# A transformer block with recurrent memory, forward and backward: buffers of a tile's input-gradient parts, two banks for the turned score gradient, casts on ScalarE, order of rows, and split loads

## The chip, the core and the metric

The kernel runs on one core of a Trainium2 chip. The core has five engines, each with its own queue of instructions taken in order: TensorE (PE; its weight loads are listed apart as PEld), VectorE (DVE), ScalarE (ACT), GpSimd (POOL) and SyncE (SP, which here only issues DMAs). They wait for one another through semaphores. The metric is the device time of one launch in microseconds (us), lower is better. PSUM, into which TensorE writes, has eight banks of 128 partitions x 512 fp32 numbers; here five are handed out under the name `ps`, two under `fx`, one under `po`.

## The reference

The launch computes the output of one transformer block and the gradients of nine inputs. Cut to what matters:

```python
def _A_ref(x, mem0, Wq, Wk, Wv, Wo, seg_len):      # S 2048, Dm 448, H 16, Dh 256, M 8, seg 32
    mem = mem0
    for s in range(n_seg):                          # 64 segments, L = M + seg_len = 40 rows each
        xs = x[:, s * seg_len:(s + 1) * seg_len, :]
        h = jnp.concatenate([mem, xs], axis=1)
        q, k, v = (einsum('btd,dhe->bhte', h, W) for W in (Wq, Wk, Wv))
        p = softmax(where(mask, einsum('bhqe,bhke->bhqk', q, k) * scale, -1e9))
        o = einsum('bhte,hed->btd', einsum('bhqk,bhke->bhqe', p, v), Wo)
        mem = o[:, :M, :]
        outs.append(o[:, M:, :])
...
h = x + _A_ref(layernorm(x), mem0, Wq, Wk, Wv, Wo, seg_len)
h2 = h + (silu(layernorm(h) @ w_gate) * (layernorm(h) @ w_up)) @ w_down
_out, _vjp = jax.vjp(_f, A_x, A_mem0, A_Wq, A_Wk, A_Wv, A_Wo, B_w_gate, B_w_up, B_w_down)
return (_out, *_vjp(grad_out))
```

All arrays are bfloat16. The memory rows of a segment come from the segment before, so the forward pass is a chain of 64 segments, and the backward pass is another, from the last segment to the first.

## The kernel before

Four stages follow one another. The **forward chain** loads all attention weights into SBUF (Wq, Wk, Wv, Wo, some 15 MB; L424 to L430), takes segment after segment, and keeps rows for the backward pass in DRAM. The **feed-forward stage** runs forward and backward of the second half, eight groups of two tiles of 128 rows. The **backward chain** goes through the segments from 63 to 0. The **tail** reads what was kept and forms the weight gradients, as long accumulations on TensorE.

Tiles are scheduled by a framework that takes instructions by priority. What stands under `k.prio.crit()` goes first; the rest is laid into the holes that the planner sees. The order of each engine's queue is fixed when the program is built. `tc.issue_after(x)` places an instruction behind x. A tile under a tag waits until one of the tag's buffers is free, that is, until every reader of an earlier tile in it has run.

One segment s of the backward chain (r is its place in its tile t of four segments; r runs 3, 2, 1, 0):

- L1163: 128 matmuls give the gradient of the attention output, transposed, in four banks; four copies (DVE, ACT, DVE, ACT) bring it to `doT`.
- L1172: 16 transposes make it token-major, in two halves; L1173 copies the halves to `dO_sb`, the first on DVE, the second on ACT.
- L1181: 32 matmuls give the gradient of the probabilities (`pD`); L1188 to L1193 on DVE form from it and the probabilities `P_sb` the score gradient `dS_bd` (prod, row sum, prod, product with the block-diagonal `P_bd`).
- `heads("v")`, `heads("k")`, `heads("q")`: 16 matmuls each (L1140, in `head_mm`) into three banks. Each bank is copied in two parts, the segment's own 32 rows into `blk` and the 8 memory rows into `lo`; the banks alternate between DVE and ACT (L1202, L1205; all `k.evac` copies show as L75 on DVE and L76 on ACT).
- between "k" and "q", L1221 turns `dS_bd` into one bank `pT`, and two copies bring its halves to `dST_bd`, which `heads("q")` needs.
- `rows_in` (L1212): 32 matmuls for each of v, k and q add the own rows into the bank `pH`; four of them lie side by side on the array.
- L1230 (DVE) and L1231 (ACT) copy `pH` to `om`; L1234 multiplies it by `sel`; L1238 writes the next segment's memory rows to `do_roll`, for which the next segment's L1163 waits; L1245 copies the remaining 24 columns into `dxT`, a buffer for the whole tile.

Not in the critical order: the load of a segment's rows (`load_seg`, L1080 to L1095: V transposed, Q and K on SP, P on POOL into one of two buffers `Pb`, and POOL's two copies into `P_bd`), the stores of `blk` and `lo` on POOL, and at r = 0 the tile's end: 96 matmuls with the memory rows (L1279, into a bank `fx`, q first, then k and v), a copy `om2` (L1282), L1286, two copies into `dxT`, four transposes of `dxT` (L1294) and a LayerNorm backward step (`ln_bwd`, L253 to L264). `lo` has two buffers for v and k and one for q.

At the start of the forward chain POOL issues the loads of Wq, Wk, Wv, Wo and of the remaining rows of x; `rest_rows(0)` (L486) copies rows on POOL as well; SP issues the first rows of x, a store of normalised rows (L459) and the mask (L194, L195), which DVE reads at L413. `rest_unit` (L475) uses two `fx` banks for each of eight units, copied by DVE and ACT.

Of the kernel before, what the change touches and what calls it, by code (L numbers as in the profile page):

```python
# [9 lines left out]
FP32 = mybir.dt.float32  # L10
BF16 = mybir.dt.bfloat16
# [4 lines left out]
P = 128  # L16
# [129 lines left out]
def run_all(k: _K):  # L146
# [17 lines left out]
    k.A = _Arena(arena, "arA", 64.5)  # L164
# [205 lines left out]
def forward_chain(k: _K):  # L370
# [52 lines left out]
    for Wd_sb, Ws, rest in ((Wq_sb, k.Wq2, 0), (Wk_sb, k.Wk2, 64), (Wv_sb, k.Wv2, None)):  # L423
        nc.gpsimd.dma_start(out=Wd_sb, in_=Ws[0:3 * P, :].rearrange("(kc p) n -> p kc n", p=P))  # L424
        if rest is not None:
            nc.gpsimd.dma_start(out=Wqk3[rest:rest + 64, :], in_=Ws[3 * P:D, :])
    for b in range(2):
        nc.gpsimd.dma_start(out=Wv3[64 * b:64 * b + 64, :].rearrange("p (m c) -> p m c", c=512), in_=v3[:, :, b])
    nc.gpsimd.dma_start(out=Wo_sb, in_=k.Wo2.rearrange("(c p) d -> p c d", p=P))
    nc.gpsimd.dma_start(out=xn_all[:, 2:NT, 0:D], in_=x_rows[:, 2:NT])  # L430
# [49 lines left out]
    def rest_rows(s):  # L480
        R = R_b[(s // 8) % 2]
        for dst, src in ((qT_b[s % 2], R[0]), (kT_b[s % 2], R[1])):
            d4 = dst.rearrange("p (c g x) n -> p g c x n", g=2, x=2)
            s4 = src[:, :, M * (s % 8):M * (s % 8) + M].rearrange("p (g c x) n -> p g c x n", g=2, x=2)
            for g in range(2):
                nc.gpsimd.tensor_copy(out=d4[:, g, :, :, 0:M], in_=s4[:, g])  # L486
# [556 lines left out]
def backward_chain(k: _K):  # L1043
# [21 lines left out]
    dh_h = [B(9.875, 448).bitcast(FP32), A(48.5, 448).bitcast(FP32)]  # L1065
    dhx = A(62.5, KC, P)
    dmr = A(63.5, KC, 16, M)
    P_bd, dS_bd, dST_bd = [B(1.25 * i, 8, 2, L) for i in range(3)]
    Pb = [B(3.75 + 0.625 * i, 8, L) for i in range(2)]
# [12 lines left out]
    def load_seg(s):  # L1082
# [8 lines left out]
        P_sb = Pb[s % 2]  # L1091
# [51 lines left out]
    for s in range(NSEG - 1, -1, -1):  # L1143
# [6 lines left out]
        P_sb = Pb[s % 2]  # L1150
# [5 lines left out]
        with k.prio.crit():  # L1156
# [11 lines left out]
            def token_major(hf):  # L1168
# [4 lines left out]
                k.evac(dO_sb[:, 8 * hf:8 * hf + 8, :], ph.rearrange("p (c n) -> p c n", n=P), "vs"[hf])  # L1173
# [19 lines left out]
            nc.vector.tensor_tensor(out=dS_bd, in0=prod.unsqueeze(2).to_broadcast([P, 8, 2, L]), in1=P_bd, op=ALU.mult)  # L1193
# [3 lines left out]
            def heads(nm, lhs, rhs):  # L1197
                pps[nm] = [k.ps1() for _ in range(3)]
                head_mm(pps[nm], lhs, rhs, nm != "v")
                for b in range(3):  # L1200
                    c0, n, v = c12(pps[nm][b], b)
                    k.evac(blk[nm][:, c0:c0 + n, r * SEG:(r + 1) * SEG], v[:, :, M:L], "vsv"[b])  # L1202
                for b in range(3):
                    c0, n, v = c12(pps[nm][b], b)
                    k.evac(lo[nm][:, c0:c0 + n, r * M:(r + 1) * M], v[:, :, 0:M], "svs"[b])  # L1205
                if s == 0:
                    k.tl.outs(*{"v": (7, 9), "k": (9, 10), "q": (10, 11)}[nm], 0, 6)


# [5 lines left out]
            heads("v", dO_sb, P_bd)  # L1215
            rows_in("v", WvT_sb, 0, MC)
            heads("k", Q_sb, dS_bd)
            pT = k.ps1()
            for h in range(8):
                for g in range(2):  # L1220
                    nc.tensor.matmul(pT[64 * g:64 * g + L, h * L:(h + 1) * L], lhsT=dS_bd[:, h, g, :],  # L1221
                                     rhs=ident[:, 64 * g:64 * g + L], start=True, stop=True, skip_group_check=True)
            for g in range(2):
                k.evac(dST_bd[64 * g:64 * g + L, :, g, :],
                       pT[64 * g:64 * g + L, 0:8 * L].rearrange("p (h n) -> p h n", n=L), "vs"[g])
            rows_in("k", WkT_sb, 0, 20)
            heads("q", K_sb, dST_bd)
            rows_in("k", WkT_sb, 20, MC)
            rows_in("q", WqT_sb, 0, MC)
            k.last_om = nc.vector.tensor_copy(out=om[:, 0:224], in_=pH[:, 0:224])  # L1230
            nc.scalar.copy(out=om[:, 224:D], in_=pH[:, 224:D])  # L1231
# [7 lines left out]
            else:  # L1239
                pm0 = k.ps1()  # L1240
                nc.tensor.matmul(pm0[0:M, 0:D], lhsT=sel[:, 24:32], rhs=om[:, 0:D], start=True, stop=True)
                dm = B(3.75, D)[0:M, :]
                nc.vector.tensor_copy(out=dm, in_=pm0[0:M, 0:D])
                nc.sync.dma_start(out=OUT2[:, :], in_=dm)
            nc.scalar.copy(out=dxT[:, :, r * SEG + M:(r + 1) * SEG], in_=pm3[:, :, 0:24])  # L1245
# [301 lines left out]
```

## Time and profile before

| | |
|---|---|
| median of 3 runs | 3059.83 us (3057.76 to 3062.02) |
| the profiled execution | 3052.22 us, span from first to last instruction 3050.5 us, mean granted TensorE clock 0.993 |
| forward chain | 0 to about 1050 us |
| feed-forward stage | about 1050 to 1344 us |
| backward chain | 1344.1 (first L1163) to 2392.6 us |
| tail | to 3050.5 us |
| busy share of the span | PE 95%, PEld 57%, DVE 45%, ACT 35%, POOL 22% |

A segment of the backward chain can be followed by the starts of L1163's first matmul: 15.90, 15.91, 16.78, 15.87 us in turn for most tiles, the third being the one with L1286 and L1294 in it. The first segment of the chain lasts 25.0 us, the next three 16.52, 15.55 and 15.93 us.

How to read the lines: in a timeline, start, length (both in us), engine, line of the kernel, operation, tile written <- tiles read, shapes, count, and in brackets how long the engine had been idle before it and what released it. Buffers are named by their arenas: `arW` (weights, loaded rows), `arA` and `arB` (work), `psf` (a bank of the tag `ps`), `omb` (`om`). A run of instructions of the same kind is one line; its length runs from the first start to the last end, so that neighbouring matmul lines overlap. Ends of matmuls are modelled; starts are measured.

### The profile page before, as it was taken

The numbers are of one execution on the slowest core, as the hardware profiler recorded it, in microseconds if no ns is written. First come the engines' busy times: TensorE is split into PE (matmuls) and PEld (weight loads), VectorE is DVE, ScalarE is ACT, GpSimd is POOL, SyncE is SP. The second block draws the span as 40 slices with busy tenths as digits, with TensorE's granted clock in tenths as the row PEclk, the third lists the DMA queues.
The fourth block names the chain that finished last, engine by engine and source line by source line (L and its number), as shares of the span: only waits on it lengthen the run. The fifth ranks groups of instructions, "written<-read, shape, count | busy, mean of one in ns | idle before, by whom it ended". The sixth has DMA issues, their size and how long they took to land.

```text
span 3050.5 us, 108244 instructions
## 1 busy us (share of the span) xinstructions
PE 2890.3 (95%) x47650; PEld 1748.7 (57%) x47650; DVE 1363.8 (45%) x3437; ACT 1052.6 (35%) x2562; POOL 685.2 (22%) x1522
## 2 busy tenths in 40 slices
PE   6899999999998999989999999999999999999999
PEld 3555555555554555556776677677767554544444
DVE  3555455555555576754555554555455201111110
ACT  2444444444444544443333333333333101111110
POOL 2222222222222232232212122122211112111111
PEclk9999999999999999999999999999999999999999
DMA  7567756776766989895446545455544898959951
GB/s 247 138 168 183 187 165 169 184 178 172 192 173 173 283 217 237 205 326 131 138 130 161 134 131 146 139 141 145 139 138 130 277 285 233 223 173 219 214 160 54
DMA packets 738650, 551.88 MB, mean 181 GB/s; under 512 B 600788, under 2 KB 633732, under 8 KB 735620
## 3 DMA queue, kind: packets, MB, share of 16 engines
q1 hardware_dynamic: 686804, 393.58, 52.5%
q0 software_dynamic: 51376, 151.38, 14.9%
q8 instruction: 374, 6.13, 0.9%
q14 instruction: 96, 0.79, 0.1%
HBM read 169.84 MB, written 236.00 MB: 133 GB/s over the span
## 4 chain that ended last, share of the span: by engine, by line
PE 76%; issue 7%; DVE 6%; DMA 5%; ACT 4%; POOL 1%; SPq 1%; ACTq 0%; POOLq 0%; DVEq 0%
PE psf L1388 8%; PE po L1212 7%; PE psf L1163 7%; PE psf L546 6%; PE psf L663 5%; PE po L708 4%; PE psf L901 4%; PE psf L1140 3%; PE fx L1279 3%; PE fx L1388 3%; PE psf L1234 2%; PE fx L475 2%; PE fx L1025 2%; DVE arA L75 2%; PE psf L560 2%
## 5 line engine op out<-in xcount | busy, mean ns | idle before, releaser
L75 DVE CAST arA<-psf 128x256 bf16<-128x256 f32 (+3 forms) x925 | 422.2, 477 | 768.2 <-PE psf L1388 249.9
L76 ACT CAST arA<-psf 128x96 bf16<-128x96 f32 (+5 forms) x923 | 359.8, 411 | 1052.0 <-PE psf L1163 223.8
L1212 PE MATMUL po<-arW,arA 128*32 128x448 bf16 x6144 | 346.6, 355 | 7.7 <-DMA arW<-Tq 5.5
L1388 PEld LDWEIGHTS <-arA 128*128 128x128 bf16 x1440 | 139.1, 98 | 161.4 <-issue 6.1
L1212 PEld LDWEIGHTS <-arA 128*32 128x32 bf16 x6144 | 158.6, 96 | 125.3 <-issue 6.5
L1163 PEld LDWEIGHTS <-arW 128*128 128x128 bf16 x8192 | 212.8, 96 | 24.0 <-issue 24.0
L1388 PE MATMUL psf<-arW,arA 128*128 128x512 bf16 x882 | 223.3, 382 | 0.0
L1163 PE MATMUL psf<-arA,arW 128*128 128x40 bf16 x8192 | 216.2, 179 | 5.5 <-DVE arA L1238 5.1
L663 PE MATMUL psf<-arW,arA 128*64 128x512 bf16 x1536 | 216.5, 382 | 0.0
L546 PE MATMUL psf<-arW,arA 128*32 128x512 bf16 x3072 | 193.6, 385 | 12.5 <-DVE arA L749 12.5
L76 ACT COPY arA<-psf 128x512 bf16<-128x512 bf16 (+3 forms) x206 | 149.2, 725 | 118.3 <-DVE arA L75 76.5
L76 ACT CAST arB<-psf 128x64 bf16<-128x64 f32 (+3 forms) x384 | 121.9, 318 | 159.7 <-PE psf L550 109.7
L708 PE MATMUL po<-arW,arA 128*32 128x256 bf16 (+1 forms) x4096 | 141.6, 263 | 10.4 <-DVE arA L75 7.7
L75 DVE COPY arA<-psf 128x512 bf16<-128x512 bf16 (+2 forms) x204 | 104.3, 512 | 99.8 <-PE psf L560 55.5
L901 PE MATMUL psf<-arW 128*128 128x256 bf16 (+1 forms) x1288 | 146.3, 274 | 1.3 <-DVE arA L967 0.7
L901 PEld LDWEIGHTS <-arW 128*128 128x128 bf16 (+1 forms) x1344 | 102.4, 97 | 51.5 <-issue 40.8
L546 PEld LDWEIGHTS <-arA 128*32 128x32 bf16 x3072 | 70.4, 96 | 90.2 <-DVE arA L749 18.1
L1140 PEld LDWEIGHTS <-arW 128*128 128x128 bf16 x2048 | 84.3, 99 | 62.1 <-issue 53.2
L1428 PE MATMUL psf<-arW 128*128 128x448 bf16 x525 | 112.1, 356 | 4.5 <-DVE arA L75 4.5
L475 PE MATMUL fx<-arA,arW 128*128 128x64 bf16 (+1 forms) x2048 | 84.2, 195 | 31.7 <-ACT arB L76 19.0
L708 PEld LDWEIGHTS <-arA 128*32 128x32 bf16 x4096 | 93.7, 96 | 32.6 <-DVE arA L75 10.9
L1465 POOL DMA_DIRECT2D out_dram<-arA x96 | 52.1, 545 | 262.6 <-DVE arA L75 237.1
(292 smaller groups left out, 4577.6 us busy)
## 6 DMA issues: line engine op xcount, KB each, us to landing
arW<-T SPq DMA_DIRECT2D x256, 128.0 KB
X_o<-arA SPq DMA_DIRECT2D x37, 512.0 KB
T<-arA SPq DMA_DIRECT2D x64, 256.0 KB
X_v<-arA POOLq DMA_DIRECT2D x30, 512.0 KB, 4.6
X_k<-arA POOLq DMA_DIRECT2D x30, 512.0 KB, 3.8
X_q<-arA POOLq DMA_DIRECT2D x30, 512.0 KB, 3.9
out_dram<-arA POOLq DMA_DIRECT2D x84, 128.0 KB, 4.2
VG<-arA SPq DMA_DIRECT2D x64, 160.0 KB
```

The costliest lines, as they stand in the source:

```text
L75: return nc.vector.tensor_copy(out=out, in_=in_)
L76: return nc.scalar.copy(out=out, in_=in_)
L475: nc.tensor.matmul(banks[w][:, i * 64:(i + 1) * 64], lhsT=lhsT, rhs=xr[lo:hi, kc, :], start=(kc == 0 and i == 0), stop=(kc == KC - 1), ski ...
L546: nc.tensor.matmul(banks[w][32 * q:32 * q + 32, :], lhsT=hT_roll[:, kc, sl, M:L], rhs=(Wq_sb, Wk_sb)[w][:, kc, col(q, b)], start=(kc == 0) ...
L663: nc.tensor.matmul(pV[b][64 * g:64 * g + 64, 0:512], lhsT=hT_flat[:, kc, sl * L:sl * L + 64], rhs=Wv_sb[:, kc, n * 512:(n + 1) * 512], sta ...
L708: nc.tensor.matmul(pO[32 * q:32 * q + 32, 0:w], lhsT=xblk[:, j, r * SEG:(r + 1) * SEG], rhs=Wo_sb[:, cj(j), 256 * dh:256 * dh + w], start= ...
L901: nc.tensor.matmul(ps[fp][:, f2 * 256:(f2 + 1) * 256], lhsT=Wt[lo:hi, kc, c * P:(c + 1) * P], rhs=xT[lo:hi, kc, :], start=(kc == 0 and f2 ...
L1140: nc.tensor.matmul(ps[b][:, i * 2 * L:(i + 1) * 2 * L], lhsT=lhs[:, at, :], rhs=rhs_bd[:, cl // 2, :, :].rearrange("p g n -> p (g n)"), st ...
L1163: nc.tensor.matmul(pss[b][:, jj * L:(jj + 1) * L], lhsT=WoT_sb[:, kc, c * P:(c + 1) * P], rhs=do_roll[:, kc, sl, :], start=(kc == 0), stop ...
L1212: nc.tensor.matmul(pH[32 * (j % 4):32 * (j % 4) + 32, 0:D], lhsT=blk[nm][:, j, r * SEG:(r + 1) * SEG], rhs=WT[:, cj(j), :], start=(nm == " ...
L1388: k.last_mm = nc.tensor.matmul(pa[i][:, 0:w], lhsT=lhs_of(b)[:, i // 2 * P:(i // 2 + 1) * P], rhs=rhs_of(q, b, i % 2), start=(b == 0), sto ...
L1428: k.last_mm = nc.tensor.matmul(pa[i][:, 0:D], lhsT=lhs_of(b, i), rhs=rhs_of(b), start=(bi == 0), stop=(bi == m + 3))
```

## The change

Eight edits, all but the last in the backward chain:

1. The parts of `dxT` for r = 3, 2, 1 go to buffers of their own (`dx3`, `dx2` in three pieces, one of them in the mask tile, `dx1`), copied from the bank in the segment that makes them; at r = 0 POOL copies all five pieces into `dxT`.
2. The third bank of `heads("q")` at r = 3 has its memory rows copied to `lq3` (in the tile `mv2`), and POOL brings them to `lo["q"]` at r = 2.
3. One buffer `P_sb` instead of two; the arena `arA` grows by 0.25 KB.
4. `dO_sb`: the first half on ACT, the second on DVE.
5. All own rows of v, and all memory rows of v, are copied on ACT; for k and q the same bank's own and memory rows stay on one engine, and the memory rows come after the turned copies.
6. The turned score gradient has two banks, one for each half.
7. 12 of the key rows instead of 20 stand before `heads("q")`; `om` is one DVE copy.
8. Start: the weight loads are split between SP and POOL; the copies of `rest_rows(0)` move from POOL to DVE.

```diff
-    for Wd_sb, Ws, rest in ((Wq_sb, k.Wq2, 0), (Wk_sb, k.Wk2, 64), (Wv_sb, k.Wv2, None)):
-        nc.gpsimd.dma_start(out=Wd_sb, in_=Ws[0:3 * P, :].rearrange("(kc p) n -> p kc n", p=P))
...
+    def chunks(eng, Wd_sb, Ws, c0, c1):
+        eng.dma_start(out=Wd_sb[:, c0:c1], in_=Ws[c0 * P:c1 * P, :].rearrange("(kc p) n -> p kc n", p=P))
+    chunks(nc.gpsimd, Wq_sb, k.Wq2, 0, 2)
+    chunks(nc.sync, Wq_sb, k.Wq2, 2, 3)
+    nc.sync.dma_start(out=Wqk3[0:64, :], in_=k.Wq2[3 * P:D, :])
+    chunks(nc.sync, Wk_sb, k.Wk2, 0, 2)
+    chunks(nc.gpsimd, Wk_sb, k.Wk2, 2, 3)
+    nc.gpsimd.dma_start(out=Wqk3[64:P, :], in_=k.Wk2[3 * P:D, :])
+    chunks(nc.gpsimd, Wv_sb, k.Wv2, 0, 2)
+    chunks(nc.sync, Wv_sb, k.Wv2, 2, 3)
     for b in range(2):
-        nc.gpsimd.dma_start(out=Wv3[64 * b:64 * b + 64, :].rearrange("p (m c) -> p m c", c=512), in_=v3[:, :, b])
-    nc.gpsimd.dma_start(out=Wo_sb, in_=k.Wo2.rearrange("(c p) d -> p c d", p=P))
-    nc.gpsimd.dma_start(out=xn_all[:, 2:NT, 0:D], in_=x_rows[:, 2:NT])
+        nc.sync.dma_start(out=Wv3[64 * b:64 * b + 64, :].rearrange("p (m c) -> p m c", c=512), in_=v3[:, :, b])
+    for c0, eng in ((0, nc.sync), (MC // 2, nc.gpsimd)):
+        eng.dma_start(out=Wo_sb[:, c0:c0 + MC // 2], in_=k.Wo2.rearrange("(c p) d -> p c d", p=P)[:, c0:c0 + MC // 2])
+    nc.sync.dma_start(out=xn_all[:, 2:NT, 0:D], in_=x_rows[:, 2:NT])
...
     def rest_rows(s):
+        eng = nc.gpsimd if s > 0 else nc.vector
...
+    dx3 = A(48, KC * 48).bitcast(FP32).rearrange("p (c n) -> p c n", c=KC)
+    lq3 = k.mv2[:].rearrange("p t n -> p (t n)").bitcast(BF16).rearrange("p (c m) -> p c m", m=M)
+    dx2 = [(A(64.5, 96).bitcast(FP32).rearrange("p (c n) -> p c n", c=2), 0, 2, P, 2),
+           (A(48.375, 48).bitcast(FP32).rearrange("p (c n) -> p c n", c=1), 2, 3, P, 2),
+           (k.maskb[:, 0:24].unsqueeze(1), 3, 4, 64, 2)]
+    dx1 = B(4.375, KC * 48).bitcast(FP32).rearrange("p (c n) -> p c n", c=KC)
+    dx_stage = [(dx3, 0, KC, P, 3)] + dx2 + [(dx1, 0, KC, P, 1)]
...
-    Pb = [B(3.75 + 0.625 * i, 8, L) for i in range(2)]
+    Pb = [B(3.75, 8, L)]
...
-                k.evac(dO_sb[:, 8 * hf:8 * hf + 8, :], ph.rearrange("p (c n) -> p c n", n=P), "vs"[hf])
+                k.evac(dO_sb[:, 8 * hf:8 * hf + 8, :], ph.rearrange("p (c n) -> p c n", n=P), "sv"[hf])
...
-                for b in range(3):
-                    c0, n, v = c12(pps[nm][b], b)
-                    k.evac(blk[nm][:, c0:c0 + n, r * SEG:(r + 1) * SEG], v[:, :, M:L], "vsv"[b])
-                for b in range(3):
-                    c0, n, v = c12(pps[nm][b], b)
-                    k.evac(lo[nm][:, c0:c0 + n, r * M:(r + 1) * M], v[:, :, 0:M], "svs"[b])
+                for b in range(2 if nm == "k" else 3):
+                    own_rows(nm, b, "s" if nm == "v" else "vsv"[b])
...
+            def first_rows(nm, after=None):
                 for b in range(3):
                     c0, n, v = c12(pps[nm][b], b)
+                    eng = "s" if after is None else "vsv"[b]
+                    with nullcontext() if after is None else tc.issue_after(after[eng].ins):
+                        late = nm == "q" and r == 3 and b == 2
+                        k.evac(lq3 if late else lo[nm][:, c0:c0 + n, r * M:(r + 1) * M], v[:, :, 0:M], eng)
...
             heads("v", dO_sb, P_bd)
+            score_grads()
+            first_rows("v")
             rows_in("v", WvT_sb, 0, MC)
             heads("k", Q_sb, dS_bd)
-            pT = k.ps1()
+            pT = [k.ps1(), k.ps1()]
...
+            with tc.issue_after(turned["v"].ins):
+                own_rows("k", 2, "v")
+            first_rows("k", turned)
+            with tc.issue_after(last_t.ins):
+                rows_in("k", WkT_sb, 0, 12)
             heads("q", K_sb, dST_bd)
-            rows_in("k", WkT_sb, 20, MC)
+            rows_in("k", WkT_sb, 12, MC)
             rows_in("q", WqT_sb, 0, MC)
-            k.last_om = nc.vector.tensor_copy(out=om[:, 0:224], in_=pH[:, 0:224])
-            nc.scalar.copy(out=om[:, 224:D], in_=pH[:, 224:D])
+            first_rows("q", turned)
+            k.last_om = nc.vector.tensor_copy(out=om[:, 0:D], in_=pH[:, 0:D])
...
-            nc.scalar.copy(out=dxT[:, :, r * SEG + M:(r + 1) * SEG], in_=pm3[:, :, 0:24])
+            if r == 3:
+                nc.scalar.copy(out=dx3, in_=pm3[:, :, 0:24])
+            elif r == 2:
+                nc.gpsimd.tensor_copy(out=lo["q"][:, 24:32, 3 * M:4 * M], in_=lq3)
+                for stg, c0, c1, n, _ in dx2:
+                    nc.scalar.copy(out=stg[0:n], in_=pm3[0:n, c0:c1, 0:24])
+            elif r == 1:
+                nc.scalar.copy(out=dx1, in_=pm3[:, :, 0:24])
+            else:
+                for stg, c0, c1, n, q in dx_stage:
+                    nc.gpsimd.tensor_copy(out=dxT[0:n, c0:c1, q * SEG + M:(q + 1) * SEG], in_=stg[0:n])
+                nc.scalar.copy(out=dxT[:, :, r * SEG + M:(r + 1) * SEG], in_=pm3[:, :, 0:24])
```

The changed kernel's `own_rows(nm, b, eng)` copies the own rows of one bank, `score_grads` is the L1193 product. In it the copies that were L1245 stand at L1276 (r = 3), L1280 (r = 2), L1282 (r = 1) and L1286 (r = 0).

## The prediction

> **What bounds the kernel now.** I read the windows by stage first. The backward chain (64 segments of L1163, 1344 to 2393 us) is over a third of the span, and PE is busy in it almost throughout:
>
> ```profile
> 1417.00:2385.00 968.00, 941.90 (x22255) 681.13 (x22251) 496.95 (x1244) 346.92 (x990) 197.98 (x447) 1.00 0.52 140
> ```
>
> The columns are length, busy us of PE, weight loads, DVE, ACT and POOL, granted clock, DMA share, GB/s. DVE (51%), ACT (36%) and the DMA engines (52%) have room, so only PE's order and what it waits for can set the time. Matmul ends are modelled, so small stalls hide inside that 97%; the timeline of one segment shows them by start times. This segment starts at 1804.81, the next at 1820.71: 15.90 us.
>
> ```profile
> 1808.67 0.69 DVE L75 COPY arA<-psf 128x1024 bf16<-128x1024 bf16 x1 [0.76 <-PE psf L1172]
> 1809.24 1.01 ACT L76 COPY arA<-psf 128x1024 bf16<-128x1024 bf16 x1 [0.54 <-PE psf L1172]
> 1809.70 1.07 PE L1140 MATMUL psf<-arB,arA 128*128 128x80 bf16 x16
> 1810.31 0.33 PEld L1140 LDWEIGHTS <-arA 128*128 128x128 bf16 x8 [0.28 <-ACT arA L76]
> 1810.66 0.62 ACT L76 CAST arA<-psf 128x384 bf16<-128x384 f32 x2 [0.41 <-PE psf L1140]
> 1810.70 0.56 PE L1279 MATMUL fx<-arW,arB 128*32 128x448 bf16 x8
> 1811.09 1.69 PE L1212 MATMUL po<-arW,arA 128*32 128x448 bf16 x32
> 1812.00 0.83 DVE L1193 TENSOR_TENSOR arB<-prod,arB 128x640 bf16<-128x640 f32 x1
> 1812.97 0.73 PE L1140 MATMUL psf<-arB,arW 128*128 128x80 bf16 x16
> 1813.99 1.31 PE L1212 MATMUL po<-arW,arA 128*32 128x448 bf16 x21
> 1814.35 0.47 DVE L75 CAST arB<-psf 40x320 bf16<-40x320 f32 x1
> 1814.91 0.42 ACT L76 CAST arB<-psf 40x320 bf16<-40x320 f32 x1 [0.40 <-DVE arB L75]
> 1815.38 0.73 PE L1140 MATMUL psf<-arB,arW 128*128 128x80 bf16 x16
> 1816.05 2.26 PE L1212 MATMUL po<-arW,arA 128*32 128x448 bf16 x43
> 1818.36 0.39 DVE L1230 COPY omb<-po 128x224 f32<-128x224 f32 x1 [1.50 <-PE po L1212]
> 1818.84 0.35 ACT L1231 COPY omb<-po 128x224 f32<-128x224 f32 x1 [1.91 <-DVE omb L1230]
> 1820.34 0.19 DVE L1238 CAST arA<-psf 128x32 bf16<-128x32 f32 x1 [1.59 <-PE psf L1234]
> ```
>
> Read it as a chain: the value heads stop for ACT's 1.01 us half of dO; the key heads wait for dS (ends 1812.83); the query heads wait for the turned dS, two copies in one bank one after the other; the next segment waits for om, the L1234 product and L1238. The L1279 matmuls (96 per tile, 32 in this segment) fill the holes. Starts give their price: four (a quad) in 0.19 us, the same for L1212. Where no fillers exist, at 1385.61, the segment is still 15.55 us: the chain decides, not the fillers.
>
> Why fillers can't spread: the four dxT parts share one buffer, so these copies stand until the tile before is turned (L1294, 1722.27), each holding one of five psum banks:
>
> ```profile
> 1723.11 0.39 ACT L1245 COPY arB<-psf 128x96 f32<-128x96 f32 x2
> ```
>
> Last, the start. POOL's queue holds the Wv rest and Wo behind a copy until 35.0 and 36.27; PE waits 2.73 us for Wo at 53.69. The mask (issued 8.98 on SP) lands at 22.3:
>
> ```profile
> 22.31 0.24 DVE L413 CAST arA<-maskb 128x160 bf16<-128x160 f32 x1 [4.22 <-DMA maskb<-mask]
> 36.27 1.71 POOL L429 DMA_DIRECT2D arW<-in_A_Wo_dram  x1
> 53.69 1.04 PE L708 MATMUL po<-arW,arA 128*32 128x256 bf16 x16 [2.73 <-DMA arW<-in_A_Wo_dram]
> ```
>
> **The change, one ordinary segment.** Times run from its first L1163; the order of each engine is that of the built program, durations are the rows above. After, fillers stand 4, 13 and 7 to a segment, about 24 in all four segments, where before they stood 32, 32, 11, 21.
> 1. Up to the value heads nothing changes: 4.89. ACT now takes the first dO half (start 1808.67 or as ACT comes free, 3.9; plus 1.01 = 4.9), DVE the second (4.43 + 0.69 = 5.12). The heads run 5.0 to 5.65; before they ended at 5.89. Gain 0.24.
> 2. Fillers: 4 (0.19), not 8 (0.39). The own value rows are all cast on ACT: the first starts 0.42 after the heads (the distance from 1815.38 to 1815.80), takes 0.48 and ends at 5.90; the second and third follow at 0.34 steps (two casts, 0.48 and 0.28, lasted 0.62). L1212 starts at 6.0, a new wait of 0.15, and ends at 7.53; with 0.17 for changing tile size, 7.70. Behind it stand the key heads, but:
> 3. DVE now runs prod, rsum, prod, dS without casts between: 5.04 + 0.49 + 0.48 + 0.48 + 0.83 with 0.03 between = 7.4. Add the 0.14 seen between 1812.83 and 1812.97: 7.55, so dS is ready before PE. Key heads at 7.70; before 8.16.
> 4. Key heads and turning take 1.02 as before: 8.72. Twelve rows wait for one key cast (7.70 + 0.42 + 0.55 + 0.1 = 8.76), then 3 quads (0.57) and 0.17: 9.50. The two turned copies lie in two banks and run side by side from 8.78 to 9.25, inside those rows. Query heads at 9.50; before 10.57, though with 8 rows (0.38) and 8 fillers (0.38) more ahead of them: 0.31 net.
> 5. Query heads 0.67, then 52 rows, 13 quads of 0.19: 12.64. om starts 0.40 later (as 1817.96 to 1818.36) and is one DVE copy of 448 columns: 0.39 for 224, and 0.14 per 128 more between the 256- and 384-column casts, so 0.63; 13.67. L1234: 0.06, then 8 records in 1.01 (0.34 for two, 0.11 each further): 14.74. L1238 starts 0.10 later, takes 0.19, PE follows 0.18 after: 15.2.
> So 15.2 against 15.90, with 8 fewer fillers (0.38): 0.32 is really saved. No bank is late by the tile-to-bank map: the latest, the value heads' second, is free at 6.8 and wanted at 8.36.
>
> **The tile-end segment** (16.78 before, 11 fillers; L1286 and L1294 in it). After, it carries 25 fillers (0.67 more), and on DVE L255 and a query cast stand between om and L1238: L253 and L255 cost 0.8 and 0.62, the cast waits for three fillers after L1234. I add: 14.1 rows done, om 15.1, L1234 to 16.2, cast 16.85, L1238 17.04, next 17.2.
>
> Tile: 3 x 15.2 + 17.2 = 62.8 against 64.45 (15.90, 15.91, 16.78, 15.87): 1.65 saved, x14 = 23.1. The first tile, without fillers, 2.2; the second (64.47 to 4 x 15.2) 3.6. At the end 2.6 is given back: tile 1's L1286/L1294 and more fillers now lie behind the last segment (10.4 us of work after its L1234, 7.3 before). Backward: **26 us**. Bounds, from +/-0.25 us in each of 64 segments (one more DVE hand-over of 0.1, one more quad): 10 to 42.
>
> **Copies added.** POOL: five dxT copies and one of lq3 per tile; nearest row L1251, 0.22 each (bound 0.45, L1095): 1.3 to 2.7 us in a 62.8 us tile in which POOL is 20% busy, covered unless rival C. On ACT L1280 is three copies (0.21 to 0.28) instead of one, once per tile, covered by the 1.86 us that ACT has at a segment's start (first copy at 1806.67); uncovered it would be 0.4 x 16 = 6 us.
>
> **Start.** Two queues: Wo no longer waits for POOL's copies. Gain at most the 2.73 wait and, if all behind it moves up, the 3.0 us in which the DMA engines stood unused behind POOL's copy (shares 0.74 and 0.67 in 30:35 and 35:40). Against it: on SP the mask now stands behind Wq, Wk and Wv parts. Packets of 8 KB move at about 390 GB/s (393 in 5:10); SP's 4.7 MB with as much from POOL need 24 us from 4, and its XN stores more: the mask lands at 28 to 33, not 22.3. DVE holds L413 ahead of the casts that free fx, so the fourth L475 unit (32.77 before) could start at 31 to 35. Loss 0 to 3, and after an idle stretch PE runs slow (32 matmuls took 1.79 us at 29.64, 1.10 at 32.77), another 2. Sum -5 to +5; I take 0. The Trainium skill, "DMA: Bandwidth & Descriptors", section "Issuing engines are not separate DMA queues", speaks against the split: queues share 16 engines and only the issue time is saved. By that rule alone the start would gain POOL's 3.0 and lose nothing, and the total would be 3 us lower; no run here tells yet.
>
> **Sum.** The profiled run took 3052.2 (span 3050.5 plus 1.7): 3052.2 - 26 = 3026. The median of the runs is 3059.8, 7.6 above it; I predict on the median: 3059.8 - 26 = **3034**.
>
> **Rivals.**
> A, less: hand-overs I count as covered are not (the 0.15 value wait and the longer om copy repeat elsewhere), or the start loses its 5: segments 15.5, tile about 64.0, 0.45 x 14 + 4 = 10 us: 3050. For it: the no-filler segment's 15.55. Against: each release above is 0.05 to 1 us early.
> B, the change doesn't do what it says: fillers only change places, tiles stay at 64.45, the 2.2 and 3.6 of the first two tiles less the 2.6 at the end remain: 3057. Against it: three waits (0.28, 0.17, 0.4) lose their cause outright.
> C, slower: one P_all buffer instead of two. Its load now waits behind POOL's lq3 copy, which waits for fillers at 12.7 of the segment: issued at 13.2, landed 3.2 later (median; longest 7.2), two L1095 copies of 0.48: 17.4, wanted by the value heads at 20.2. It decides from a landing of 6.0; to be slower than before all 15 tiles need 1.75 lost, a landing of 7.8. At 8.5, 15 x (1.65 - 2.5) = 13 slower: 3072.
> D, more: the start gains 5 and tile-end segments 0.6 each: 3019.
>
> **Chances.** Forecast 0.58, A 0.20, D 0.09, B 0.06, C 0.07. Range 3014 to 3053: the backward bounds and start, cutting B and C off. About 0.2% (6 us) is what can be told from no change: faster 0.86 (forecast, D, nearly all of A), same 0.07, slower 0.07.
>
> **What would show it.** Segment starts 15.2 apart; no wait of the value heads for ACT; turned copies overlapping; L1245's successors each in its own segment; L413 at 28 or later and no 2.7 wait for Wo. I am wrong if PE waits for POOL L1095's copy or P_all, if the tile-end segment exceeds 18, or if L1234 waits for om longer than 0.5.

## The result, and the profile after

| | before | after |
|---|---|---|
| median of the runs | 3060.93 us (3057.76 to 3067.38, 4 runs) | 3018.89 us (3016.28 to 3034.08, 4 runs) |
| profiled execution, span | 3052.22, 3050.5 us | 3018.94, 3017.1 us |
| ordinary backward segment | 15.90 us | 14.88 us |
| segment with the tile's end | 16.78 us | 17.20 us |
| tile of four segments | 64.45 us | 61.86 us |

The ratio of the times is 0.9878, with an interval of 0.9855 to 0.9901. In a second set of runs, on another occasion, the changed kernel took 3024.64 us (3022.11 to 3026.67) against 3063.31: 0.9865 (0.9843 to 0.9888). By ratios and medians the change saves 37 to 42 us; the two intervals together reach from 30 to 48. The two profiled executions differ by only 33.4, since that of before lay 8.7 below the median given here (7.6 below the earlier one) and that of after on its median.

Where the 33.4 us of the two traces lie, by the starts of the backward segments:

| stretch | before | after | saved |
|---|---|---|---|
| up to the first L1163 / L1178 | 1344.1 | 1346.6 | -2.5 |
| first tile | 73.0 | 71.6 | 1.4 |
| second tile | 64.5 | 60.9 | 3.6 |
| third tile (no tile's end in it after the change) | 64.5 | 59.5 | 5.0 |
| the next twelve tiles | 775.3 | 744.1 | 31.2 |
| last tile, up to its last segment | 48.6 | 47.0 | 1.6 |
| from there to the end | 680.6 | 687.5 | -6.9 |

(The column adds up to 33.4. Up to the last segment's start the chain itself saves 42.8; 2.5 are lost ahead of it and 6.9 behind.)

The stage row shows what the busy share can tell: windows of the changed kernel over the backward chain, in the same columns as the row of before (length, busy us of PE, weight loads, DVE, ACT, POOL, clock, DMA share, GB/s).

```profile
1418.00:2345.00 927.00, 917.76 (x22222) 662.66 (x22215) 483.29 (x1177) 355.27 (x1014) 212.84 (x532) 1.00 0.54 147
```

PE went from 97% to 99% of the stretch; DVE works 14 us less in it, ACT 8 and POOL 15 more. More is seen in the timeline of one ordinary segment of the changed kernel. It starts at 1818.80, the next at 1833.68: 14.88.

```profile
1822.71 1.01 ACT L76 COPY arA<-psf 128x1024 bf16<-128x1024 bf16 x1
...
1823.78 0.75 PE L1155 MATMUL psf<-arB,arA 128*128 128x80 bf16 x16
...
1824.73 1.70 PE L1235 MATMUL po<-arW,arA 128*32 128x448 bf16 x32
...
1825.44 0.83 DVE L1209 TENSOR_TENSOR arB<-prod,arB 128x640 bf16<-128x640 f32 x1
...
1826.42 0.73 PE L1155 MATMUL psf<-arB,arW 128*128 128x80 bf16 x16
...
1827.49 0.48 DVE L75 CAST arB<-psf 40x320 bf16<-40x320 f32 x1
1827.58 0.42 ACT L76 CAST arB<-psf 40x320 bf16<-40x320 f32 x1
...
1828.12 0.75 PE L1155 MATMUL psf<-arB,arW 128*128 128x80 bf16 x16
...
1831.27 0.92 PE L1320 MATMUL fx<-arW,arA 128*32 128x448 bf16 x13
1831.50 0.62 DVE L1261 COPY omb<-po 128x448 f32<-128x448 f32 x1 [1.76 <-PE po L1235]
...
1832.18 1.08 PE L1264 MATMUL psf<-sel,omb 128*128 128x32 f32 x8
...
1833.57 0.24 ACT L1282 COPY arB<-psf 128x96 f32<-128x96 f32 x1 [4.19 <-DVE arA L1268]
```

TensorE no longer stops ahead of any of the three heads (L1155), or inside one. The score gradient (L1209) ends at 1826.27, before TensorE wants it; the two turned copies run side by side inside twelve key rows; the dxT part (L1282) leaves its bank in the segment that makes it. The waits of TensorE between 1500 and 2250 us say the same, first before, then after (us in total, times, longest):

```profile
PE psf L1140 <- DVE arB L1193: 6.0, 14, 0.4
PE psf L1163 <- DVE arA L1238: 3.4, 12, 0.3
```

```profile
PE fx L1335 <- ACT arB L1331: 3.9, 12, 0.3
```

The wait for the score gradient is gone but for one of 0.3, that for the next memory rows (L1238, now L1268) altogether; a new one of 0.3 per tile stands in the tile's end. These totals list only holes over 0.15 us, so they name the places and are no measure of the gain.

The start changed its shape, not its length. Timeline of the changed kernel:

```profile
36.55 0.24 DVE L413 CAST arA<-maskb 128x160 bf16<-128x160 f32 x1 [11.09 <-DMA maskb<-mask]
37.78 1.71 PE L482 MATMUL fx<-arA,arW 128*128 128x64 bf16 x31 [5.64 <-DVE arW L75]
54.67 0.84 PE L716 MATMUL po<-arW,arA 128*32 128x256 bf16 x16 [0.42 <-DVE arA L75]
```

The wait for Wo (2.73) is gone, but the mask lands 14 us later than before and holds DVE, so the fourth unit of L482 waits 5.64. The second segment starts at 60.31 (59.80 before), the third at 77.37 (77.56 before).

### The profile page after: what moved, and what is told of

Read it like the earlier page. It is cut to its first block, busy times and chain, and to the rows that moved or that the text cites. A ratio compares the mean times of both kernels' runs of the same rounds, so it can differ in the third digit from the quotient of the medians.

```text
span 3017.1 us, 108283 instructions
## 1 busy us (share of the span) xinstructions
PE 2868.7 (95%) x47650; PEld 1733.5 (57%) x47650; DVE 1352.5 (45%) x3377; ACT 1062.2 (35%) x2594; POOL 697.0 (23%) x1610
## 4 chain that ended last, share of the span: by engine, by line
PE 81%; issue 7%; DMA 4%; DVE 3%; ACT 3%; POOL 1%; SPq 1%; POOLq 0%; ACTq 0%; DVEq 0%
PE po L1235 10%; PE psf L1429 8%; PE psf L1178 7%; PE psf L554 6%; PE psf L671 5%; PE po L716 4%; PE psf L1155 4%; PE psf L909 3%; PE fx L1320 3%; PE fx L1429 3%; PE fx L482 2%; PE fx L1033 2%; PE psf L1264 2%; PE psf L568 2%; PE psf L1187 2%
## 5 line engine op out<-in xcount | busy, mean ns | idle before, releaser
L76 ACT CAST arA<-psf 128x384 bf16<-128x384 f32 (+6 forms) x1051 | 397.3, 423 | 922.8 <-PE psf L1429 215.2
L75 DVE CAST arA<-psf 128x256 bf16<-128x256 f32 (+6 forms) x797 | 355.7, 471 | 712.2 <-PE psf L1429 249.9
L1235 PE MATMUL po<-arW,arA 128*32 128x448 bf16 x6144 | 327.6, 355 | 4.1 <-DVE arA L75 2.1
L1178 PEld LDWEIGHTS <-arW 128*128 128x128 bf16 x8192 | 211.5, 96 | 23.3 <-issue 18.4
L1178 PE MATMUL psf<-arA,arW 128*128 128x40 bf16 x8192 | 217.4, 180 | 0.8 <-DVE arA L1268 0.8
L1235 PEld LDWEIGHTS <-arA 128*32 128x32 bf16 x6144 | 146.9, 96 | 118.2 <-ACT arA L76 9.3
L76 ACT CAST arB<-psf 128x64 bf16<-128x64 f32 (+1 forms) x320 | 108.3, 339 | 150.5 <-PE psf L558 106.7
L554 PEld LDWEIGHTS <-arA 128*32 128x32 bf16 x3072 | 70.5, 96 | 89.7 <-DVE arA L757 18.1
L482 PE MATMUL fx<-arA,arW 128*128 128x64 bf16 (+1 forms) x2048 | 84.4, 195 | 36.7 <-ACT arB L76 19.0
L1469 PE MATMUL psf<-arW 128*128 128x448 bf16 x525 | 111.6, 352 | 3.1 <-DVE arA L75 1.7
L716 PEld LDWEIGHTS <-arA 128*32 128x32 bf16 x4096 | 94.4, 97 | 30.2 <-DVE arA L75 11.1
L1155 PEld LDWEIGHTS <-arW 128*128 128x128 bf16 x2048 | 80.0, 100 | 52.3 <-issue 51.1
```

The lines of the kernel that those rows point to most:

```text
L75: return nc.vector.tensor_copy(out=out, in_=in_)
L76: return nc.scalar.copy(out=out, in_=in_)
L482: nc.tensor.matmul(banks[w][:, i * 64:(i + 1) * 64], lhsT=lhsT, rhs=xr[lo:hi, kc, :], start=(kc == 0 and i == 0), stop=(kc == KC - 1), ski ...
L554: nc.tensor.matmul(banks[w][32 * q:32 * q + 32, :], lhsT=hT_roll[:, kc, sl, M:L], rhs=(Wq_sb, Wk_sb)[w][:, kc, col(q, b)], start=(kc == 0) ...
L716: nc.tensor.matmul(pO[32 * q:32 * q + 32, 0:w], lhsT=xblk[:, j, r * SEG:(r + 1) * SEG], rhs=Wo_sb[:, cj(j), 256 * dh:256 * dh + w], start= ...
L1155: nc.tensor.matmul(ps[b][:, i * 2 * L:(i + 1) * 2 * L], lhsT=lhs[:, at, :], rhs=rhs_bd[:, cl // 2, :, :].rearrange("p g n -> p (g n)"), st ...
```

## The experiments

All are edits of the changed kernel but e5. "Ordinary" and "tile's end" are the usual lengths of these segments in the run's profile, without the half-clock stretches told of below.

| run | median, us (range) | ratio to before (interval) | ordinary | tile's end |
|---|---|---|---|---|
| e1 one dxT | 3076.32 (3060.04 to 3090.98) | 1.0042 (1.0018 to 1.0066) | 14.88 | 18.95 |
| e2 one turned bank | 3042.09 (3037.01 to 3050.37) | 0.9937 (0.9919 to 0.9956) | 15.08 | 16.84 |
| e3 dO halves as before | 3030.11 (3028.74 to 3038.21) | 0.9895 (0.9864 to 0.9926) | 14.98 | 17.43 |
| e4 value casts as before | 3043.85 (3039.67 to 3064.77) | 0.9949 (0.9919 to 0.9979) | 15.42 | 16.07 |
| e5 before, with the buffers | 3057.40 (3048.90 to 3068.91) | 0.9986 (0.9971 to 1.0001) | 15.90 | 16.30 |
| e6 om in two halves | 3030.54 (3026.88 to 3053.29) | 0.9911 (0.9883 to 0.9939) | 15.06 | 17.59 |
| e7 old start | 3025.38 (3017.06 to 3038.19) | 0.9887 (0.9854 to 0.9920) | 14.88 | 17.20 |
| e8 mask copy written later | 3025.57 (3017.67 to 3041.91) | 0.9891 (0.9851 to 0.9931) | 14.88 | 17.20 |
| e9 mask behind the casts | 3015.79 (3010.23 to 3021.44) | 0.9837 (0.9811 to 0.9863) | 14.88 | 17.20 |
| e10 one dxT, one turned bank | 3072.10 (3063.05 to 3080.34) | 1.0022 (1.0005 to 1.0039) | 15.08 | 19.57 |
| e11 4 key rows | 3032.70 (3026.59 to 3049.31) | 0.9900 (0.9862 to 0.9939) | 15.05 | 17.38 |
| e12 the changed kernel again | 3024.64 (3022.11 to 3026.67) | 0.9865 (0.9843 to 0.9888) | 14.88 | 17.20 |

Each ratio is to runs of the kernel before that were taken beside it: their median was 3060.07 us for e1 to e4, 3062.61 for e5 to e8 and 3063.31 for e9 to e12. The part of edit 5 that places the memory rows of k and q behind the turned copies, and edits 2 and 3 within the changed kernel, were not undone one by one.

**e1, one dxT.**

```diff
-            if r == 3:
-                nc.scalar.copy(out=dx3, in_=pm3[:, :, 0:24])
...
+            nc.scalar.copy(out=dxT[:, :, r * SEG + M:(r + 1) * SEG], in_=pm3[:, :, 0:24])
```

> The changed kernel, but the parts of dxT for r = 3, 2, 1 go straight into the one dxT again, so their copies wait until the tile before is turned and each holds a bank until then. Theory (hand-overs): the gain comes from three shorter hand-overs in each segment (turned copies, score gradient, dO halves); held banks cost nothing, and fillers only change places (24, 36, 15, 21 in the four segments instead of 25, 24, 24, 23). Tile 61.8 to 62.2 us against 61.9, and the tile's end comes back into its own tile (3 to 4 us less behind the last segment): 3012 to 3023 against 3019. Rival (buffers): the held banks were the price; then a tile goes back towards 64.45 and the kernel to 3045 or more.

The theory fell. The rival's time came (3045 or more), and the kernel is even slower than before; but its reason, tiles back at 64.45, is only half of it. The segments without held banks keep 14.88, so the hand-overs are as short as ever; the loss is in the tile's end. Timeline of e1, in the segment that starts at 1844.64:

```profile
1854.64 1.09 PE L1318 MATMUL fx<-sel,om 128*128 128x32 f32 x8 [0.64 <-ACT om L1314]
...
1856.05 1.12 PE L1326 MATMUL fx<-identf,arB 128*128 128x128 f32 x4 [0.33 <-ACT arB L1322]
...
1857.21 0.38 ACT L1277 COPY arB<-psf 128x96 f32<-128x96 f32 x2 [1.13 <-PE fx L1326]
...
1857.50 0.57 PE L1246 MATMUL psf<-ident,arB 128*40 128x40 bf16 x16 [0.33 <-ACT arB L1277]
...
1863.39 1.08 PE L1264 MATMUL psf<-sel,omb 128*128 128x32 f32 x8 [0.73 <-DVE omb L1261]
```

The turning (L1246) waits for the two held copies (L1277), which wait for the tile to be turned (L1326). The changed order makes it so: the key banks' memory rows are copied only after the turned copies, so with two banks held the key heads have the last three, and no bank is left for the turning until the tile's end is done. That end then stands bare on TensorE between key heads and turning, waiting for ScalarE three times (0.64, 0.33, 0.33), and its LayerNorm work on DVE meets om (0.73). A tile is 64.47 at best (14.84, 14.88, 15.80, 18.95), 2.6 more, some 37 us in 14 tiles. What the tiles of this trace take above 64.47, 18 us together, goes mostly with the clock; windows of e1:

```profile
1852.70:1856.10 3.40, 2.43 (x34) 1.72 (x33) 0.56 (x1) 1.32 (x4) 1.38 (x3) 1.00 0.52 144
1856.10:1859.50 3.40, 3.07 (x37) 1.78 (x38) 1.11 (x4) 1.57 (x6) 0.00 (x0) 0.50 0.41 161
```

A stretch in which TensorE was busy for 2.43 of 3.40 us is followed by one at half clock: the twelve key rows in it took 1.24 us, not 0.68. The trace of e1 has twelve such stretches between 1421 and 2392 us, that of the changed kernel none there; with one, the tile's end is 20.1 to 21.7 long.

**e2, one bank for the turned score gradient.**

```diff
-            pT = [k.ps1(), k.ps1()]
+            pT = [k.ps1()] * 2
```

> The changed kernel, but the turned score gradient lies in one bank again. Theory (hand-overs): the two copies run one after the other as before (1.03 us from the first one's start to the query heads, at 8.69 of the segment), so the query heads start at 9.72 instead of 9.32: 0.40 per segment, 62 segments, +25 us: 3040 to 3048 against 3019. Rival: twelve key rows and the other work hide most of it, or the planner puts fillers into the hole and takes them away elsewhere: less than 0.15 per segment, 3019 to 3028.

The kernel's time is as expected, the segment's is not: 15.08, 0.20 more, not 0.40. Timeline of e2, segment from 1828.96:

```profile
1837.66 0.48 DVE L75 CAST arB<-psf 40x320 bf16<-40x320 f32 x1
...
1838.23 0.42 ACT L76 CAST arB<-psf 40x320 bf16<-40x320 f32 x1 [0.55 <-DVE arB L75]
...
1838.71 0.73 PE L1155 MATMUL psf<-arB,arW 128*128 128x80 bf16 x16
```

The copies do follow one another and the query heads start at 9.75 of the segment, as expected (9.72), but the planner put 17 rows instead of 12 into the hole, which gives 0.2 back behind them. The other half of the loss is that the fillers crowd (12 and 36 instead of 25 and 24): tile's end 16.84, but the next segment 16.33.

**e3, dO halves on the engines of before.**

```diff
-                k.evac(dO_sb[...], ph..., "sv"[hf])
+                k.evac(dO_sb[...], ph..., "vs"[hf])
```

> The changed kernel, but the first half of dO on VectorE and the second on ScalarE as before. The order of every engine is otherwise the same. Theory: the value heads end 0.24 later (5.89 of the segment as before against 5.65) and everything behind them moves with it: 0.24 x 63 = 15 us, 3030 to 3037. Rival: the 0.24 is absorbed, because the rows of v wait for their cast and the key heads for the score gradient anyway: less than 0.08 per segment, under 3024.

The time lies at the theory's lower edge (11 us above the changed kernel's first runs, 5 above its second), the segment between the two. Timeline of e3, segment from 1827.93:

```profile
1832.36 1.01 ACT L76 COPY arA<-psf 128x1024 bf16<-128x1024 bf16 x1 [0.55 <-PE psf L1187]
...
1832.82 1.07 PE L1155 MATMUL psf<-arB,arA 128*128 128x80 bf16 x16
...
1834.02 1.69 PE L1235 MATMUL po<-arW,arA 128*32 128x448 bf16 x32
```

The heads start earlier (4.89) and last 1.07 instead of 0.75, as the second half stops them until 1833.4; the value rows start at 6.09 instead of 5.93. The first value cast already runs behind the first eight heads, so 0.16 of the 0.24 is left there, and 0.10 at the segment's end; in the tile's end 0.23.

**e4, value casts as before.**

```diff
-            heads("v", dO_sb, P_bd)
             score_grads()
+            heads("v", dO_sb, P_bd)
...
-                    own_rows(nm, b, "s" if nm == "v" else "vsv"[b])
+                    own_rows(nm, b, "vsv"[b])
...
-                    eng = "s" if after is None else "vsv"[b]
+                    eng = "svs"[b] if after is None else "vsv"[b]
```

> The changed kernel, but the value banks are cast as before: own rows on VectorE, ScalarE, VectorE, memory rows right behind on the other engine, and the score-gradient product ahead of them in the program. Theory: VectorE carries casts between the steps of the score gradient again, the key heads start at 8.0 to 8.16 of the segment instead of 7.62, so 0.35 to 0.54 per segment, +22 to +34, less 4 because the fillers fall back to the old places (32, 32, 11, 21) and less work lies behind the last segment: 3036 to 3049. Rival: the casts on VectorE fit between its waits and ScalarE's cast was the later one: less than 0.15 per segment, 3012 to 3026.

The theory held: 15.42, 0.54 more. Timeline of e4, the tile-end segment from 1833.55, DVE's part and the key heads (in the ordinary segment before it the key heads start at 8.17):

```profile
1838.96 0.55 DVE L75 CAST arA<-psf 128x384 bf16<-128x384 f32 x1
...
1840.55 0.25 DVE L75 CAST arA<-psf 128x96 bf16<-128x96 f32 x1
1840.74 0.82 DVE L1209 TENSOR_TENSOR arB<-prod,arB 128x640 bf16<-128x640 f32 x1
...
1841.71 0.73 PE L1155 MATMUL psf<-arB,arW 128*128 128x80 bf16 x16 [0.25 <-DVE arB L1209]
```

Three casts stand between the steps of the score gradient, and the key heads start at 8.16 of the segment, as before the change (7.62 after it). The fillers fall back to 32, 32, 11, 21 and the tile's end costs only 0.65 more than an ordinary segment (2.32 in the changed kernel), so a tile at its usual lengths is 62.27, only 0.41 more. The profiled span is 30 us longer than the changed kernel's: 3.7 ahead of the chain, 7 in the first three tiles, 13 in the next twelve (5 of it by the usual lengths, the rest in single longer segments) and 7 behind the last segment's start. So the 0.54 is shown; that it makes the 25 us of the medians (19 against e12) is not.

**e5, the kernel before with edits 1 to 3 alone.** The buffers, lq3 and the single P buffer as in the change's diff, in the old order.

```diff
-    Pb = [B(3.75 + 0.625 * i, 8, L) for i in range(2)]
+    Pb = [B(3.75, 8, L)]
...
-            nc.scalar.copy(out=dxT[:, :, r * SEG + M:(r + 1) * SEG], in_=pm3[:, :, 0:24])
+            if r == 3:
+                nc.scalar.copy(out=dx3, in_=pm3[:, :, 0:24])
```

> The kernel before with edits 1 to 3 alone: buffers of their own for the dxT parts and the last q rows, one P buffer. TensorE's order is the one of before. Without the buffers the changed kernel lost 57 us, so: theory (together): the order of before has its tile-end work where the held banks cost nothing, the buffers are needed only by the new order, and alone they bring nothing: 3054 to 3064, segments of 15.9 and 16.8 us. Rival (buffers alone): the held banks cost here too; segments 15.5 or less, 3040 or less. A slower kernel (3066 or more) would mean that the one P buffer or POOL's copies cost.

As the revised theory has it, alone they bring nothing that these runs can separate from zero (the interval reaches 1.0001). The ordinary segments stay at 15.90; the tile's end goes from 16.78 to 16.30, which would be 7 us in 15 tiles, and 5 were measured.

**e6, om in two halves.**

```diff
-            k.last_om = nc.vector.tensor_copy(out=om[:, 0:D], in_=pH[:, 0:D])
+            k.last_om = nc.vector.tensor_copy(out=om[:, 0:224], in_=pH[:, 0:224])
+            nc.scalar.copy(out=om[:, 224:D], in_=pH[:, 224:D])
```

> The changed kernel, but om is copied in two halves, VectorE then ScalarE. Theory: the halves run one after the other as before (0.39, then 0.35 with 0.09 between: 0.83 against 0.62), so L1264 starts 0.2 later in each segment, 15.08 instead of 14.88: +13 us, 3029 to 3035. Rival: the halves overlap, or L1264 starts on the first half: 0 to 0.2 gained per segment, 3006 to 3020.

The theory held in size (15.06, 0.18 more). Timeline of e6:

```profile
1833.38 0.39 DVE L1261 COPY omb<-po 128x224 f32<-128x224 f32 x1 [1.89 <-PE po L1235]
1833.82 0.30 PEld L1265 LDWEIGHTS psf<-sel,omb 128*128 128x128 f32 x2 [0.37 <-DVE omb L1261]
...
1833.86 0.34 ACT L1262 COPY omb<-po 128x224 f32<-128x224 f32 x1 [2.59 <-DVE omb L1261]
```

The product does start on the first half, a matter of two of its eight records, but its end hangs on the second, which waits for the first.

**e7, the old start.**

> The changed kernel with the start of before: all weights on POOL's queue, the copies of the first rows on POOL. Theory: what the split gains at Wo (2.7 wait gone) it loses at the mask (5.6 wait of the fourth unit), sum within 1 us: the third segment's first L554 at 77 to 78.5 in both, whole kernel 3015 to 3023. Rival: the split is worth 3 us or more of the gain: third segment at 80 or later, 3022 or more.

```diff
-    chunks(nc.gpsimd, Wq_sb, k.Wq2, 0, 2)
-    chunks(nc.sync, Wq_sb, k.Wq2, 2, 3)
...
+        nc.gpsimd.dma_start(out=Wd_sb, in_=Ws[0:3 * P, :].rearrange("(kc p) n -> p kc n", p=P))
...
-        eng = nc.gpsimd if s > 0 else nc.vector
+        eng = nc.gpsimd
```

No difference beyond the spread of the runs: 3025.38 against 3018.89 and 3024.64, a little above the theory's range. The second segment starts at 57.83 and, in the trace of before, 59.80 us with the old loads, at 60.31 and 59.49 in the two traces with the split ones. The third starts at 75.06, earlier than either side had it (77.37 and 76.55 with the split loads), and the last forward segment at 1016.92 against 1019.29 and 1018.62. So no run shows a gain by the split; these three traces have it 1.5 to 2.5 us slower.

**e8 and e9, the mask's copy placed behind the casts.** In e8 the copy was written behind `rest_rows(0)`; the planner left it ahead of the casts, the fourth unit still waited (7.52 us), and the run tells nothing of the question. In e9 it is placed behind a cast by name:

```diff
-    nc.vector.tensor_copy(out=maskt.rearrange("p (h n) -> p h n", n=L), in_=maskb[:]...)
...
+            op = k.evac(R[w][:, 4 * u:4 * u + 4, :], ..., "vs"[w])
+            if m == 0 and u == 4 and w == 0:
+                with tc.issue_after(op.ins):
+                    nc.vector.tensor_copy(out=maskt.rearrange("p (h n) -> p h n", n=L), in_=maskb[:]...)
```

> The changed kernel, but the copy of the mask (L413) stands behind the first rows' units on VectorE instead of ahead of them. Theory: the 5.6 wait of the fourth unit was VectorE standing at the mask; without it the unit starts at 32.2 instead of 37.8, the slow clock after the idle stretch goes too, and the third segment starts at 71.5 to 74.5 instead of 77.4: 3012 to 3016. Rival: the weights are the next wait (half of Wo lands at 42.9, Wv at 34.9), and the third segment stays at 76 or later: 3017 to 3020.

> The changed kernel with the mask's copy placed behind VectorE's cast of the fifth of the eight units (in the run before, the copy kept its place ahead of the casts and the wait stayed). Theory: the 5.6 us wait of the fourth unit's matmuls goes; it starts at 32 instead of 37.8, and the second segment's first L554 at 56 to 57.5 instead of 60.3; the whole kernel 3 to 4 us less than the changed kernel beside it. Rival: Wo or Wv takes the wait's place (half of Wo lands at 42.9) and the second segment stays at 59 or later: within 1 us.

The median of e9 is 8.9 us below that of the changed kernel beside it (3015.79 against 3024.64; each of the four runs of e9 lies below each of the four of e12, though the intervals of their ratios overlap), and 47.5 us below before. Timeline of e9:

```profile
35.58 0.25 DVE L487 CAST arA<-maskb 128x160 bf16<-128x160 f32 x1 [1.45 <-DMA maskb<-mask]
...
36.81 1.05 PE L481 MATMUL fx<-arA,arW 128*128 128x64 bf16 x31 [0.53 <-DVE arW L75]
...
54.14 1.48 PE L556 MATMUL psf<-arW,arA 128*32 128x512 bf16 x24 [0.27 <-DVE arA L759]
```

Of 5.6 us waiting 0.53 is left, and the second segment starts at 54.14, 5.3 and 6.2 earlier than in the two traces of the changed kernel: more than the 3 to 4 expected, and no other load took the wait's place. This lead is still there at the last forward segment (1013.49 against 1018.62 and 1019.29). The profiled executions as a whole don't show it (spans of 3019.7 against 3020.3 and 3017.1 us): in that of e9 the feed-forward stage ran 10.24 us at half clock from 1216.5, in the other two 3.41. So some 5 to 6 us are shown, and what is left of the 8.9 isn't placed. By its median this is the fastest kernel of the study.

**e10, one dxT and one turned bank.** Both edits, of e1 and e2, together.

> The changed kernel with one dxT and with one bank for the turned score gradient: two parts undone, of which the first alone cost 57 us and the second alone 23. Theory (five banks): with one dxT two banks are held in the segment of the tile's end, three are left, the key heads take them, and a turned gradient in two banks then forces the tile's end (L1318, L1326) between key heads and turning, where TensorE waits for ScalarE copies. With one bank this goes: tile end with 27 fillers as its own stretch, ordinary segments 15.1, tile 62.5 to 63.5, 3034 to 3048, faster than with the first part undone alone. Rival (held banks cost in themselves): the costs add, 3085 or more.

Neither: 3072.10, about the time of e1. The tile's end stays between key heads and turning (19.57). The theory had miscounted: the key heads take the three banks that are left, so the turning has none even if it wants one only.

**e11, 4 key rows ahead of the query heads.**

```diff
-            rows_in("k", WkT_sb, 0, 12)
+            rows_in("k", WkT_sb, 0, 4)
```

> The changed kernel with 4 key rows instead of 12 ahead of the query heads. Theory: the rows cover the turned copies (8.69 to 9.2 of the segment) and twelve is just enough; with 4 the rows end at 8.83, TensorE waits until 9.3, and the eight rows (0.38) now come after: 0.36 more per segment, 15.24, 62 segments, +22: 3036 to 3044. Rival: the number of rows is free (the score-gradient path decides elsewhere): under 0.1 per segment, 3016 to 3025.

Slower, by half of what was expected: 15.05, 0.17 more. The planner set further rows into the hole, the query heads start at 9.32 as in the changed kernel, and one quad more stands behind them. So the rows do cover the turned copies; their number as written is not the number that runs.

**e12, the changed kernel again.**

> The changed kernel unaltered, on the same chip as the others. Theory: 14.88 per ordinary segment and 17.2 with the tile's end again; 3016 to 3024, and the distance to the kernel before 38 to 45 as in the first comparison. Rival (one profiled execution of before was a lucky one only there): the distance is nearer the 33 of the two profiled executions.

14.88 and 17.2 again. The distance of 38.7 us lies at the lower edge of the theory's 38 to 45; the time itself is 0.6 above its range.

## Why the prediction was right, and where its sizes were off

The hand-overs went as forecast, and the time lay in the range, 15 us under the number. Of these 15, 7.4 lie between the two traces (33.4 saved, not 26) and 7.6 in the offset told of last. Rival D's number, 3019, is met by luck, as its reasons are not. What the prediction missed is the part of the buffers. Term by term:

- **Value heads, casts on ScalarE, score gradient (steps 1 to 3).** Forecast: value rows at 6.0 of the segment, key heads at 7.70; measured 5.93 and 7.62. e3 and e4 show both edits at work (0.10 and 0.54 per segment when undone). The 0.24 of step 1 was too much as a term by itself, as the first cast covers part of it.
- **Turned copies and rows (step 4).** Forecast 9.50, measured 9.32. The wait of the twelve rows for a key cast (8.76) does not occur: they start at 8.64.
- **om (step 5).** Its 0.62 was right (0.63), its start was not. The 0.40 in the trace of before runs from the start of the last quad of rows; the prediction added it to the end of that quad, so 0.18 was counted twice. In the changed kernel om starts 0.23 behind the end, 0.41 behind the last start.
- **Together** these make 14.88 instead of 15.2: 0.32 in three segments of each of 14 tiles, 13 us. That is the size that was off, and the main reason why the chain saved 42.8 where 28.9 was forecast. Undone one by one, the four parts (e2, e3, e4, e6) cost 0.20, 0.10, 0.54 and 0.18 in the ordinary segment: 1.02, which is just 15.90 - 14.88. That this is so exact is partly luck: fillers change places in e2 and e4, and by whole tiles the same four cost 1.5, 0.5, 0.4 and 0.8, 3.2 together where the change saves 2.6. Each part is shown to matter; that they are independent links of one chain is not.
- **Tile's end.** Forecast 17.2 with its parts (om to 15.1, cast 16.85, L1238 17.04); measured 15.03, 17.01, 17.11 and 17.20, though with a wait of 0.33 (L1335 for ScalarE) that the forecast did not have. Forecast for the end 2.6 given back; measured 6.9. The last segment's query heads stand for 1.5 us (0.9 to 1.1 in the traces of e7, e9 and e12) for which the profile has no cause but "issue", and two tiles' ends lie behind the last product, so that the tail's long run (L1469) starts 27.4 us after that segment's start, 22.7 before. The remaining 2.2 are spread over the tail and were not traced. Against this, the third tile has no tile's end (5.0 saved instead of 1.65).
- **The buffers.** The prediction had them only let the fillers spread. e1 shows that the change does not work without those for `dxT`: the new order then costs 52 to 57 us more, and is no faster than the kernel before. e5 shows that without the new order they bring little. Neither follows from the other's price; the link, the key banks that stay full until the turned copies are done, could have been read in the code.
- **Start.** Taken as 0 in a range of 5 either way: right within the spread of the runs, and by the traces of e7 a loss of 1.5 to 2.5. The mask landed at 36.55, later than the 28 to 33 forecast, the fourth unit at 37.78 instead of 31 to 35; the gain at Wo made up for part of it. e9 shows what was to be had there.
- **Rivals.** A, with segments of 15.5, fell with 14.88. C fell at its first step: the load of P is issued at 5.8 of the segment, ahead of the lq3 copy (13.2), and lands at 9 to 10.5, 9 us early. B fell with the three waits. D's gain came, but not at its places: not from the start, nor from shorter tile's ends.
- **The offset.** Forecast on the median of before, 7.6 above its profile. The profile of after lies on its median. That the executions of before that were timed had more half-clock stretches than the profiled one would explain it; no trace of them exists, so this is open.

## What to carry to other kernels

When a chain of hand-overs decides, cost each edit by the start times of the instructions that follow it, and say from which of two starts a gap is counted. Before a buffer is called a mere freedom for fillers, count the banks that the new order keeps full at its fullest point: the worth of a buffer and the worth of an order may exist only together. And look at what stands ahead in the queue of the engine that casts: one copy that waits for a late DMA cost more here than splitting all the weight loads gained.

## What the runs showed of the hardware

Half-clock stretches of TensorE follow short holes, not only long ones. In the third segment the same instructions run in both kernels, behind the same holes of 0.58, 0.33 and 0.6 us, but after the change with the clock at 0.50. Windows of before, then of after:

```profile
89.10:92.50 3.40, 2.44 (x72) 1.77 (x72) 1.31 (x6) 1.19 (x5) 0.63 (x2) 1.00 0.50 70
```

```profile
89.10:92.50 3.40, 3.21 (x62) 2.62 (x64) 1.04 (x5) 0.67 (x3) 0.45 (x2) 0.50 0.50 70
```

This stretch alone put the changed kernel from 0.2 us ahead (third segment) to 1.3 behind (fourth, 94.85 against 93.60); that is over half of the 2.5 us lost ahead of the backward chain, and it says nothing of the change. The Trainium skill, "TensorE: Matmul & The Clock Gate", Part 1 (the clock gate), says that the clock is halved after an idle window of about 3.4 us and that such windows run freely. The length agrees (the records here are 3.4 us or a multiple); the condition of that section does not: in e1 a window with 2.43 busy of 3.40 us, its holes 0.64 and 0.33 long, was enough, in some of the tiles and not in others. In such tiles a cluster of waits of some 1.3 us cost 1.2 us or more again (18.95 against 20.11 and above). Which windows are hit is not known from these traces.

A small transfer behind large ones waits for them: the mask, issued at 9.47 on SP behind parts of Wq, Wk and Wv, landed at 36.55 in the changed kernel (36.14 in its second trace); before, with SP's queue free of weights, it was issued at 8.98 and landed at 22.3, and in e7, with the old loads again, at 23.24.
